# Batch 1's transposes in PSUM tiles of their own, and its visits moved: block-causal attention with a gated FFN on one core

## The chip, the cores and the metric

The kernel runs on one core of a Trainium2 chip. The metric is device time in microseconds (us), the median of several runs of the same program. A core has a matrix engine (PE, with a separate weight load, PEld), a vector engine (DVE), an activation engine (ACT), a general engine (POOL) and a synchronisation engine (SP) that here only issues DMAs. The engines run side by side; each takes its own instructions in order, and they wait for one another on semaphores. Matmul results land in PSUM, which DVE and ACT empty into the on-chip SBUF.

## The reference

```
q, k, v: [8 batches, 8 heads, 576, 64] f32
scores = q @ k^T / 8, masked so that a row of block i (64 rows) sees blocks j <= i
attn   = softmax(scores);  o = attn @ v
x      = o as [8*576, 512]                   # heads side by side
out    = (relu(x @ w_gate) * (x @ w_val)) @ w_out   # 512 -> 1536 -> 512, f32 out
```

## The kernel before, in words

**Tiling.** A batch has 576 rows: four chunks of 128 (the "mains") and a tail of 64. The FFN takes 512 rows of a batch at a time (the four chunks), with a ninth pass at the end for the tails of all eight batches. Heads go in pairs: round `r` is batch `r // 4`, pair `hp = r % 4`. All matmuls are bf16.

**One long FFN, with attention set into it.** `ffn_gen` (L579) is a generator that issues one 512-column FFN matmul at each step: for each batch 96 steps of gate and val products (L585; 12 column blocks `f`, four gate and four val matmuls each, then a relu on ACT, L595, and a product on DVE, L601, which gives `hT`), then 48 steps of output products (L646; four groups of 12, each copied to `ob` by DVE, L656, and stored). A batch of FFN is 144 steps. Around it the order is written out by hand: `run(base, events)` (L796) sorts a list of (position, function) and issues FFN steps up to the whole part of each position before it calls the function. So position 96 means: after FFN step 95 of this batch. The order of every engine's instructions is the order of these calls; no scheduler changes it.

**A visit** (L381) is the attention of one round: scores of the four chunks in three parts. The third part has a half in a `one` tile and a half in an `ffnp` tile, and the first and second part have an `sc` tile each. Three exponentials on ACT follow (L410 for the third part, L404 for the other two; the last one at a position of its own). `corners` (L459) zeroes masked corners, `head_av` (L517) multiplies one head's weights with v (10 matmuls, L508) and normalises on DVE (L473, L474), and `to_xT_pe` (L546) transposes the result for the FFN.

**PSUM** has three pools: `psum_sc` with two tiles of [128, 2, 512] f32 (`sc`), `psum_one` with one tile (`one`), and `psum_ffn` with three tiles (`ffnp`). A tile that is asked for waits until the last reader of the buffer's former tile is done. `ffnp` serves the gate and val products, the output groups, half of each third part, the products with v and the transposes of x; so those share three buffers.

**Batch 1's q and k** have to be transposed before its visits (rounds 4 to 7). While batch 0's FFN runs, POOL, DVE and ACT cast them to bf16 (L168), and `pe_mains` (L232) transposes one head pair on PE: four 128x128 transposes for q and four for k (L239) into PSUM, then one cast for each into `qTm` and `kTm` (L248), q on DVE and k on ACT. For pairs 0 to 2, `mains_1` (L868) hands in one `sc` tile whose two halves hold q and k; for pair 3 `pe_mains` takes two `ffnp` tiles. Round 4 + hp needs the casts of pair hp.

Positions before: pair 0 at 91, pair 1 at 92, visit of round 4 at 96, of round 5 at 112, round 4's products with v at 120, pair 2 at 122, round 4's x transposes at 125, visit of round 6 at 126, round 5's products at 128, pair 3 at 130, round 5's x transposes at 132, visit of round 7 at 138. At position 128 `mains_2(0)` also starts casts on POOL and loads on SP for batch 2, which is transposed by DMA and put in order by `un` (L856).

Of the kernel before, what the change touches and what calls it, by code (L numbers as in the profile page):

```python
# [11 lines left out]
BF = mybir.dt.bfloat16  # L12
# [5 lines left out]
def kernel(  # L18
# [26 lines left out]
    psum_sc = ctx.enter_context(  # L45
        tc.tile_pool(name="psum_sc", bufs=2, space=bass.MemoryType.PSUM)
    )
    psum_one = ctx.enter_context(
        tc.tile_pool(name="psum_one", bufs=1, space=bass.MemoryType.PSUM)
    )  # L50
# [287 lines left out]
    def cast_w(sts, eng):  # L338
        for dst, st in sts:
            eng(dst, st)  # L340
# [40 lines left out]
    def visit(r):  # L381

        b, hp = divmod(r, 4)
        at = attnT[r % 4]
        first = psum_sc.tile([128, 2, 512], FP, name="sc")
        second = psum_sc.tile([128, 2, 512], FP, name="sc")
        third = thirds()
        for c, hh in [(c, hh) for c in (2, 0, 1, 3) for hh in range(2)]:
            where = {
                0: first[:, hh, :],  # L390
                1: second[:, hh, 0:384],
                3: second[:, hh, 384:512],
                2: third[hh],
            }
            nc.tensor.matmul(  # L395
                where[c].rearrange("p (c n) -> p c n", n=128),
                kTm[b % 2][head_of(hh), c, hp, :],
                qTm[b % 2][head_of(hh), c:4, hp, :],
                start=True,
                stop=True,  # L400
            )

        def exp(sc, lo):
            return lambda: nc.scalar.activation(  # L404
                at[:, :, lo : lo + 512], sc, AF.Exp, scale=scale
            )

        def exp_third():
            for hh in range(2):
                nc.scalar.activation(  # L410
                    at[:, hh, 1024:1280], third[hh], AF.Exp, scale=scale
                )

        return exp_third, exp(first, 0), exp(second, 512)
# [44 lines left out]
    def corners(r, zero):  # L459

        at = attnT[r % 4]
        for lo, n in ((0, 512), (896, 128)):
            two = at[64:128, :, lo : lo + 2 * n].rearrange("p g (c n) -> p g c n", c=2)
            zero(two[:, :, :, 0:64])
# [4 lines left out]
    def normalise(out, av):  # L469
        n = av.shape[1]  # L470
        rows = av.shape[0]
        recip = sb.tile([128, NCH], FP, name="recip", bufs=4)[0:rows, 0:n]
        nc.vector.reciprocal(recip, av[:, :, 64])  # L473
        nc.vector.tensor_tensor(  # L474
            out=out,
            in0=av[:, :, 0:64],
            in1=recip.to_broadcast([rows, n, 64]),
            op=AX.mult,
        )
# [24 lines left out]
    def products_with_v(b, h, at, av):  # L504
        for p in range(4):
            for c in range(p + 1):
                col = BASE[c] + 128 * (p - c)
                nc.tensor.matmul(  # L508
                    av[:, p, :],
                    at[:, col : col + 128],  # L510
                    v_bf[b % 2][:, c, h, :],
                    start=(p == 0),
                    stop=(c == p),
                    skip_group_check=True,
                )

    def head_av(r, hh):  # L517
        b, hp = divmod(r, 4)
        h = 2 * hp + hh
        at = attnT[r % 4]  # L520
        if hh == 0:
            xnats[r] = sb.tile([128, 4, 128], BF, name="xnat", bufs=3)
        xnat = xnats[r]
        if b > 0 or hh == 1:
            av = psum_ffn.tile([128, 4, 65], FP, name="ffnp")
        else:
            av = psum_one.tile([128, 4, 65], FP, name="one")
        products_with_v(b, h, at[:, hh, :], av)
        normalise(xnat[:, :, 64 * hh : 64 * hh + 64], av)

    def both_av(r):

        b, hp = divmod(r, 4)
        xnats[r] = sb.tile([128, 4, 128], BF, name="xnat", bufs=3)
        for hh in range(2):
            sc = psum_sc.tile([128, 2, 512], FP, name="sc")
            av = sc[:, 0, 0:260].rearrange("q (p e) -> q p e", e=65)
            products_with_v(b, 2 * hp + hh, attnT[r % 4][:, hh, :], av)
            normalise(xnats[r][:, :, 64 * hh : 64 * hh + 64], av)
# [155 lines left out]
    dve, act, pool = nc.vector.tensor_copy, nc.scalar.copy, nc.gpsimd.tensor_copy  # L695
# [7 lines left out]
    with tc.manual_schedule(engines={E.PE, E.DVE, E.Activation, E.Pool, E.SP}):  # L703
# [28 lines left out]
        part(2, 0)  # L732
        part(2, 1)
        head_av(0, 0)
        head_av(0, 1)
        part(2, 2)
        e0.cast_v(4, 2, pool)
        corners(2, zero_pool)
        head_av(1, 0)
        part(3, 0)  # L740
        to_xT_pe(0, dve)
# [19 lines left out]
        e1, e2 = Early(1), Early(2)  # L761
# [39 lines left out]
        def round_at(p, r, av, to_xT, after=(6, 13)):  # L801

            exps = []

            def begin():
                exps.extend(visit(r))
                exps[0]()
                exps[1]()

            return [  # L810
                (p, begin),
                (p + after[0], lambda: exps[2]()),
                (min(p + after[1], av[0] - 0.5), lambda: corners(r, zero_dve)),
                *(
                    [(av[0], lambda: both_av(r))]
                    if av[1] is None
                    else [(av[i], lambda i=i: head_av(r, i)) for i in range(2)]
                ),
                (to_xT[0], lambda: to_xT[1](r)),
            ]  # L820

        def tail_at(p, b, av):
            exps = []
            x = sb.tile([64, 512], BF, name="xtail", bufs=2)

            def begin():
                exps.extend(tail_visit(b))
                exps[0]()
                exps[1]()

            def end():
                tail_av(b, 1, x)
                tail_to_xT(b, x)

            return [
                (p, begin),
                (p + 6, lambda: exps[2]()),
                (av[0], lambda: tail_av(b, 0, x)),
                (av[1], end),
            ]  # L840
# [18 lines left out]
        def mains_2(h0):  # L859
            e2.load_v_chunks(h0 // 4)  # L860
            e2.cast_qk(h0, 4, (pool, pool))
            e2.transpose(h0 // 4)
# [2 lines left out]
            e2.load_tails((0, 1))  # L865
            e2.load_tails((2,))

        def mains_1(hp, evac=(dve, act)):  # L868
            two = psum_sc.tile([128, 2, 1024], BF, name="sc")
            e1.pe_mains(hp, evac, [two[:, t, 0:512] for t in range(2)])  # L870

        events = round_at(96, 4, (120, 120.1), (125, pe_xT), (6, 11))
        events += round_at(112, 5, (128, 128.1), (132, pe_xT), (4, 14))
        events += round_at(126, 6, (138.2, 139), (146, pe_xT), (4, 9))
        events += round_at(138, 7, (148, None), (153, pe_xT), (3, 8))
        events += [
            (67, lambda: cast_w(halves[1:], act)),
            (80, lambda: e1.cast_qk(0, 4, (None, dve))),
            (91, lambda: mains_1(0)),
            (92.5, lambda: mains_1(1)),  # L880
            (112.05, lambda: cast_w(last_w[1:], dve)),
            (122.5, lambda: mains_1(2)),
            (130, lambda: e1.pe_mains(3, (dve, act))),
            (128, lambda: mains_2(0)),
            (142, lambda: e0.pe_tails((dve, act))),
            (142, lambda: e1.pe_tails((dve, act))),
# [4 lines left out]
        events = tail_at(24, 0, (37, 39)) + tail_at(40, 1, (55, 58))  # L891
# [15 lines left out]
        for b in range(3, B):  # L907
            events = tail_at(120, b, (136, 140))
            if b == 3:
                events += tail_at(3, 2, (21, 25))  # L910
            for i, p in enumerate((27, 50, 73, 96) if b == 3 else (2, 32, 62, 92)):
                r = 4 * b + i
# [43 lines left out]
```

The softmax here doesn't subtract the row's maximum and nothing guards it: scores larger than these inputs give would overflow.

## Time and profile before

| what | value |
|---|---|
| median of five runs | 366.93 us (366.25 to 367.38) |
| profiled execution, its own time | 367.36 us |
| its span in the profile | 365.3 us |
| busy: PE, DVE, ACT, POOL | 98%, 46%, 46%, 31% of the span |
| granted TensorE clock | 1.00 |
| share of PE in the chain that ended last | 96% |

The profile shows one execution. A line of the timeline has the start (us from the span's start), the duration, the engine, the source line, the operation, what it writes and reads, how many instructions were merged, and in brackets the idle time before it and what released it. Matmuls are pipelined: one of 512 columns takes 0.38 us from start to end, but the next starts 0.22 us after it, so PE's rows overlap, and "busy 98%" does not mean that PE never stood still. A wait of PE shows as a start that comes later than the pitch of the matmuls ahead of it gives. The table of waits counts only idle time between rows, so it gives less than the true standing of PE; it does give the name of what was waited for.

### The profile page before, as it was taken

What the parts mean: (1) busy time and instruction counts of PE and PEld (TensorE: products, weight loads), DVE (VectorE), ACT (ScalarE), POOL (GpSimd) and SP (SyncE); (2) the same over time, 40 slices, a digit from 0 to 9 for tenths busy, and PEclk for the clock granted to TensorE, in tenths of its full rate; (3) what the DMA queues carried; (4) which work ended last, traced back from release to release, by engine and by line L of the source; (5) the groups of instructions that cost most, each with busy time, mean ns of one, the idle gap of its engine ahead of it and who ended that gap; (6) DMA issues with size and microseconds to landing.
All of it is one profiled execution on the core that took longest, in us unless ns stands there. A gap on an engine that the chain in (4) does not pass through costs nothing.

```text
span 365.3 us, 7455 instructions
## 1 busy us (share of the span) xinstructions
PE 357.0 (98%) x2963; PEld 176.9 (48%) x2963; DVE 168.3 (46%) x393; ACT 168.5 (46%) x278; POOL 113.7 (31%) x147
## 2 busy tenths in 40 slices
PE   7999999999999999999999999999999999999995
PEld 3544445554554545444544455445544454444443
DVE  4753555465535544454354534553355434333332
ACT  4834565577245733664256634554455333302310
POOL 5676656399119100760058002900000000000000
PEclk9999999999999999999999999999999999999999
DMA  8999999999999972999369982998100320020013
GB/s 253 286 357 373 315 243 300 237 98 134 145 197 137 149 149 80 76 123 187 117 45 149 144 140 49 141 134 158 64 17 14 74 81 0 0 88 29 0 45 102
DMA packets 150339, 49.58 MB, mean 136 GB/s; under 512 B 132768, under 2 KB 143264, under 8 KB 150304
## 3 DMA queue, kind: packets, MB, share of 16 engines
q0 software_dynamic: 70320, 8.85, 51.7%
q1 hardware_dynamic: 74704, 31.08, 42.6%
q10 hardware_dynamic: 5280, 9.18, 7.9%
q8 instruction: 23, 0.38, 0.4%
q14 instruction: 12, 0.10, 0.1%
HBM read 37.75 MB, written 9.44 MB: 129 GB/s over the span
## 4 chain that ended last, share of the span: by engine, by line
PE 96%; DVE 2%; ACT 1%; issue 0%; POOL 0%; ACTq 0%; POOLq 0%
PE ffnp L585 51%; PE ffnp L646 26%; PE ffnp L508 5%; PE sc L395 3%; PE ffnp L488 3%; PE one L395 2%; PE sc L352 1%; PE sc L429 1%; PE ffnp L239 1%; PE ffnp L691 1%; DVE qTm L248 1%; PE sc L585 0%; PE one L429 0%; PE one L508 0%; DVE xnat L474 0%
## 5 line engine op out<-in xcount | busy, mean ns | idle before, releaser
L601 DVE TENSOR_TENSOR hT<-gate_sb,ffnp 128x512 bf16<-128x512 bf16 x106 | 72.8, 687 | 95.5 <-PE ffnp L585 75.4
L595 ACT ACTIVATE gate_sb<-ffnp 128x512 bf16<-128x512 f32 x108 | 64.7, 601 | 100.6 <-PE ffnp L585 100.6
L585 PE MATMUL ffnp<-xT,wg 128*128 128x512 bf16 x384 | 103.7, 379 | 0.1
L646 PE MATMUL ffnp<-wo,hT 128*128 128x512 bf16 (+1 forms) x444 | 101.4, 373 | 0.2 <-DVE ob L656 0.2
L585 PE MATMUL ffnp<-xT,wv 128*128 128x512 bf16 x376 | 101.0, 379 | 0.0
L585 PEld LDWEIGHTS <-wg 128*128 128x128 bf16 x432 | 40.2, 98 | 46.3 <-issue 4.0
L585 PEld LDWEIGHTS <-wv 128*128 128x128 bf16 x432 | 39.9, 98 | 45.5 <-issue 2.3
L646 PEld LDWEIGHTS <-hT 128*128 128x128 bf16 x444 | 40.9, 98 | 42.0 <-issue 1.1
L404 ACT ACTIVATE attnT<-sc 128x1024 bf16<-128x1024 f32 x56 | 56.9, 1039 | 0.0
L282 POOL DMA_DIRECT2D q_bf<-in_q_dram x20 | 17.7, 902 | 94.8 <-DVE hT L601 79.9
L656 DVE COPY ob<-ffnp 128x512 f32<-128x512 f32 (+1 forms) x37 | 25.0, 677 | 41.5 <-PE ffnp L646 41.5
L508 PEld LDWEIGHTS <-attnT 128*128 128x128 bf16 x640 | 26.0, 98 | 14.5 <-DVE xnat L474 3.8
L473 DVE RECIPROCAL recip<-ffnp 128x4 f32<-128x4 f32 (+1 forms) x73 | 13.1, 179 | 35.5 <-PE ffnp L508 23.4
L508 PE MATMUL ffnp<-v_bf,attnT 128*128 128x65 bf16 x570 | 26.4, 194 | 0.0
L410 ACT ACTIVATE attnT<-one 128x256 bf16<-128x256 f32 x28 | 10.8, 384 | 32.6 <-PE ffnp L395 30.1
L474 DVE TENSOR_TENSOR xnat<-ffnp,recip 128x256 bf16<-128x256 f32 x57 | 24.2, 424 | 2.0
L282 POOL DMA_DIRECT2D v_bf<-in_v_dram x25 | 21.4, 932 | 0.2 <-PE ffnp L508 0.2
L450 ACT ACTIVATE attnTt<-one 64x256 bf16<-64x256 f32 x8 | 3.0, 377 | 36.0 <-PE ffnp L429 36.0
L282 POOL DMA_DIRECT2D k_bf<-in_k_dram x20 | 17.7, 939 | 0.0
L395 PE MATMUL sc<-qTm,kTm 64*128 64x512 bf16 (+1 forms) x168 | 17.2, 305 | 0.4 <-ACT kTm L248 0.4
L395 PEld LDWEIGHTS <-kTm 64*128 64x128 bf16 x224 | 9.2, 94 | 16.2 <-issue 11.7
L441 ACT ACTIVATE attnTt<-sc 128x1024 bf16<-128x1024 f32 x16 | 15.7, 1014 | 0.0
(89 smaller groups left out, 244.9 us busy)
## 6 DMA issues: line engine op xcount, KB each, us to landing
out_dram<-ob ACTq DMA_DIRECT2D x32, 256.0 KB, 2.9
stage<-in_moe_w_gate_dram SPq DMA_DIRECT2D x6, 512.0 KB, 9.3
stage<-in_moe_w_val_dram SPq DMA_DIRECT2D x6, 512.0 KB, 9.6
stage<-in_moe_w_out_dram SPq DMA_DIRECT2D x6, 512.0 KB, 10.3
q_bf<-in_q_dram POOLq DMA_DIRECT2D x20, 128.0 KB, 4.7
k_bf<-in_k_dram POOLq DMA_DIRECT2D x20, 128.0 KB, 5.5
v_bf<-in_v_dram POOLq DMA_DIRECT2D x20, 128.0 KB, 6.3
stage<-in_v_dram SPq DMA_DIRECT2D x19, 128.0 KB, 4.8
```

Of the source, the lines that this page charges most:

```text
L282: ins = nc.gpsimd.dma_start(dst, src[b, :, 128 * c : 128 * c + n, :].rearrange("h p d -> p h d"),)
L395: nc.tensor.matmul(where[c].rearrange("p (c n) -> p c n", n=128), kTm[b % 2][head_of(hh), c, hp, :], qTm[b % 2][head_of(hh), c:4, hp, :], ...
L404: return lambda: nc.scalar.activation(at[:, :, lo : lo + 512], sc, AF.Exp, scale=scale)
L441: return lambda: nc.scalar.activation(at[:, :, 2 * i : 2 * i + 2, 0:256], main[i].rearrange("p g (h n) -> p g h n", h=2), AF.Exp, scale=scale,
L473: nc.vector.reciprocal(recip, av[:, :, 64])
L474: nc.vector.tensor_tensor(out=out, in0=av[:, :, 0:64], in1=recip.to_broadcast([rows, n, 64]), op=AX.mult,)
L508: nc.tensor.matmul(av[:, p, :], at[:, col : col + 128], v_bf[b % 2][:, c, h, :], start=(p == 0), stop=(c == p), skip_group_check=True,)
L585: nc.tensor.matmul(to, (wg, wv)[t][f // 4][:, c, 128 * (f % 4) : 128 * (f % 4) + 128], x[:, c], start=(c == 0), stop=(c == 3),)
L595: nc.scalar.activation(gate_sb, gate, AF.Relu)
L601: nc.vector.tensor_tensor(out=h, in0=gate_sb, in1=val, op=AX.mult)
L646: nc.tensor.matmul(op, hT[f][:, 128 * s : 128 * (s + 1)], wo[f // 4][:, f % 4, n0:n1], start=(f == 0), stop=(f == 11),)
L656: nc.vector.tensor_copy(ob, op)
```

## The change

- Pairs 0 to 2: q and k get a PSUM tile each instead of the halves of one `sc` tile: pair 0's q in `one`, its k and both of pairs 1 and 2 in `sc` tiles. Pair 3 leaves `ffnp`: its q and k lie side by side in one `one` tile (a single bank).
- Positions: pairs 0 to 3 at 89, 91, 121.5 and 128.5 instead of 91, 92.5, 122.5 and 130. Round 5's products with v at 129 instead of 128 and its x transposes at 134 instead of 132. The visit of round 6 at 127 instead of 126 (its last exponential and its corners, whose positions are relative, move by one with it).
- The product with v of round 4's first head is in the `one` tile instead of an `ffnp` tile.

```diff
@@ head_av
-        if b > 0 or hh == 1:
+        if (b > 0 or hh == 1) and (r, hh) != (4, 0):
             av = psum_ffn.tile([128, 4, 65], FP, name="ffnp")
         else:
             av = psum_one.tile([128, 4, 65], FP, name="one")
@@ mains_1 and the list of events
-        def mains_1(hp, evac=(dve, act)):
-            two = psum_sc.tile([128, 2, 1024], BF, name="sc")
-            e1.pe_mains(hp, evac, [two[:, t, 0:512] for t in range(2)])
+        def mains_1(hp):
+            if hp == 3:
+                both = psum_one.tile([128, 1024], BF, name="one")
+                two = [both[:, 512 * t : 512 * t + 512] for t in range(2)]
+            else:
+                two = [
+                    psum_one.tile([128, 1024], BF, name="one")[:, 0:512]
+                    if (hp, t) == (0, 0)
+                    else psum_sc.tile([128, 2, 1024], BF, name="sc")[:, 0, 0:512]
+                    for t in range(2)
+                ]
+            e1.pe_mains(hp, (dve, act), two)
 
         events = round_at(96, 4, (120, 120.1), (125, pe_xT), (6, 11))
-        events += round_at(112, 5, (128, 128.1), (132, pe_xT), (4, 14))
-        events += round_at(126, 6, (138.2, 139), (146, pe_xT), (4, 9))
+        events += round_at(112, 5, (129, 129.1), (134, pe_xT), (4, 14))
+        events += round_at(127, 6, (138.2, 139), (146, pe_xT), (4, 9))
         events += round_at(138, 7, (148, None), (153, pe_xT), (3, 8))
...
-            (91, lambda: mains_1(0)),
-            (92.5, lambda: mains_1(1)),
+            (89, lambda: mains_1(0)),
+            (91, lambda: mains_1(1)),
             (112.05, lambda: cast_w(last_w[1:], dve)),
-            (122.5, lambda: mains_1(2)),
-            (130, lambda: e1.pe_mains(3, (dve, act))),
+            (121.5, lambda: mains_1(2)),
+            (128.5, lambda: mains_1(3)),
             (128, lambda: mains_2(0)),
```

## The prediction, made before the result was known

> **What bounds the kernel now.** I read the page first, then PE's waits, then the chain of waits between 38 and 62 us, then the timeline of that stretch.
>
> ```profile
> span 365.3 us, 7455 instructions
> PE 96%; DVE 2%; ACT 1%; issue 0%; POOL 0%; ACTq 0%; POOLq 0%
> ...
> 299.29 20.72 PE ffnp L585 x96
> ```
>
> PE carries 96% of the chain. The last line is from the chain in order of time: 96 matmuls of 512 columns in 20.72 us, so one starts every 0.216 us. That is my ruler: where PE starts later than its ruler says, it stood still. The change touches only 39 to 61 us (batch 1's visits), and its worth is the standing there. The table of waits names the waits; the timeline gives their sizes.
>
> ```profile
> PE sc L395 <- ACT kTm L248: 0.4, 1, 0.4
> PE one L395 <- ACT kTm L248: 0.3, 1, 0.3
> PE ffnp L646 <- DVE ob L656: 0.2, 1, 0.2
> PE ffnp L239 <- DVE xnat L474: 0.2, 1, 0.2
> ...
> ACT kTm L248 <- DVE qTm L248: 4.4, 2, 2.3
> ```
>
> ```profile
> 39.88 1.35 DVE L248 COPY qTm<-sc 128x512 bf16<-128x512 bf16 x2 [0.34 <-PE sc L239]
> ...
> 40.60 0.59 ACT L248 COPY kTm<-sc 128x512 bf16<-128x512 bf16 x1 [2.09 <-DVE qTm L248]
> ...
> 41.42 0.38 PE L395 MATMUL sc<-qTm,kTm 64*128 64x512 bf16 x2
> 41.57 0.59 ACT L248 COPY kTm<-sc 128x512 bf16<-128x512 bf16 x1
> ...
> 42.22 0.40 PE L395 MATMUL sc<-qTm,kTm 64*128 64x384 bf16 x4 [0.42 <-ACT kTm L248]
> ...
> 48.69 0.69 DVE L656 COPY ob<-ffnp 128x512 f32<-128x512 f32 x1 [0.17 <-PE ffnp L646]
> ...
> 49.44 0.59 PE L646 MATMUL ffnp<-wo,hT 128*128 128x512 bf16 x2 [0.17 <-DVE ob L656]
> ...
> 51.24 0.59 ACT L248 COPY kTm<-sc 128x512 bf16<-128x512 bf16 x1 [2.33 <-DVE qTm L248]
> ...
> 51.88 0.28 PE L395 MATMUL one<-qTm,kTm 64*128 64x256 bf16 x1 [0.32 <-ACT kTm L248]
> ...
> 54.26 0.38 PE L239 MATMUL ffnp<-ident,q_bf 128*128 128x128 bf16 x4
> ...
> 54.80 0.38 PE L239 MATMUL ffnp<-ident,k_bf 128*128 128x128 bf16 x4 [0.16 <-DVE xnat L474]
> ...
> 55.86 1.46 PE L646 MATMUL ffnp<-wo,hT 128*128 128x512 bf16 x6
> ```
>
> The reader is to see that a k cast on ACT starts when the q cast on DVE ends (39.88+0.69=40.57, then 40.60), because both come from one `sc` tile, and that a visit then waits for k. PE's standing by the ruler: 0.58 at 42.22 (the pair at 41.42 is fed by 41.64); 0.33 at 49.44 (20 products from 48.49 at 0.030 end at 49.10; `ob`'s buffer comes free at 49.38); 0.48 at 51.88 (51.18+0.22=51.40); 0.25, 0.33 and 0.18 at 54.26, 54.80 and 55.86 (`ffnp` buffers held by av and by the casts). Sum 2.15 us. Every visit also starts 0.10 late with nothing waiting (55.86+6x0.216=57.16, the start is 57.25); that stays.
>
> **The change part by part.** No instruction is added or removed; SP's and POOL's order is unchanged, and no DMA belongs to a moved step. Costs come from moved waits alone. Positions count FFN matmuls.
>
> *Head pairs 0 and 1* (positions 89 and 91 for 91 and 92). q0 goes to `one`, k0 and the later ones to `sc` tiles of their own. Position 88's matmul starts at 38.58, so q0 runs 38.80-39.02 and k0 to 39.25 (eight transposes take 0.45: 39.23 to 39.68 in the trace). k0's cast waits for PE alone: last transpose 39.19 + 0.26 (the lag of before: 39.62 to 39.88) = 39.45, to 40.04. After two matmuls q1 runs 39.68-39.90. k1 needs the `sc` buffer that k0's cast holds: a new wait, 40.10 - 39.90 = 0.19. No row shows it; at least 0 (if the cast starts at once), at most 0.3 (if k0's cast is tied to q0's DVE cast, which starts at 39.54 behind the hT product). I take 0.19. Behind it on PE queue the gate's last matmul and four val matmuls, and hT, which is no later than now (41.7 against 41.89). k1's cast runs 40.5-41.1, the q casts end at 40.92, and the visit starts at 41.50 with everything free: its second `sc` pair, late by 0.58 now, waits for nothing. Net 0.58 - 0.19 = 0.39.
>
> *(4,0)'s product in `one`.* The out group that follows no longer takes the buffer of the second `ob` copy but of the first (47.83-48.52). 0.33 goes. `one` is free there: its exponential ended at 46.80.
>
> *Head pair 2* (121 for 122), *third visit* (127 for 126). DVE sets the pace: `ob` 48.69-49.38, two av normalisations to 50.47, q cast 50.51-51.20. The k cast now runs beside it, and two more matmuls lie between: PE reaches the visit 0.12 after the q cast. 0.48 - 0.10 = 0.38 goes. POOL's k cast of heads 4 and 5 (47.88-48.50, fed by DMA) is needed at 49.1 instead of 50.0: cover 0.6.
>
> *Head pair 3* (128 for 130), q and k in one bank, (5,0) and (5,1) at 129, xT at 134. With 1.12 gained by then, visit 6 starts at 50.98 and its third exponential leaves `one` at 51.74 (0.38 + 0.38 after the start, as at 51.88 now). PE comes to the transposes at 51.84: no wait, with cover 0.05. The products of (5,0) and (5,1) stand behind them. On DVE the q cast now stands ahead of their normalisations: cast 52.49-53.18, the first done at 53.80, the second at 54.34. The next out group (due 53.76) and the xT transposes (due 54.3) wait for these: I take 0.32 together. Low end 0.1 (if q's cast starts after its own four), high end 0.8 (one cast of 0.69 more). Now 0.25+0.33+0.18 = 0.76, so net 0.44.
>
> *A rule against this part.* Row: at 55.22 the k cast of pair 3 ran beside the q cast (54.68-55.37), from two tiles; pairs 0 to 2 ran one after the other though each half has a bank of its own. The Trainium skill ("PSUM — Partial Sum Buffer", section "PSUM bank collisions raise a hardware error") says that two engines must not touch one bank and quadrant at once, reads included, and that different banks are clean. So the old wait was the tile's, not the bank's, while the new single bank forces ACT behind DVE. By the old row k3's cast would run 52.5-53.1; by the rule 53.2-53.8, and the visit's second 1.04 us exponential behind it on ACT ends at 54.9. The sum is the same by both: the last visit, at 55.7, wants that `sc` buffer at 55.9, cover 1.0. After it ACT has a store to issue (0.35) and xT (0.59) before the last visit's first exponential at 56.1: cover 0.3. Without cover it would cost up to 0.7. The store and a load exchange completion slots; both slots' earlier transfers had been read by 53.2, so 0.
>
> *Behind 61 us* PE is dense. One thing does not move with it: DMA. DVE's third unpermute (76.20) would come at 74.7, and its transfer lands at about 75.1 (landing events). DVE waits 0.5; its next work for PE is the tail's reciprocal, which waits 1.61 for PE (78.40). 0. Batch 3's k lands at 109.3, and its visit comes at 111.8: cover 2.5.
>
> Sum: 0.39+0.33+0.38+0.44 = 1.54. The profiled execution took 367.36 (span 365.3 and 2.06 around it), which becomes 365.8; it lies 0.43 over the median of the five runs, 366.93, which becomes 365.4. With the bounds (0 to 0.3, 0.1 to 0.8) the gain is 1.0 to 1.95, so 365.0 to 365.9; a median's own scatter (runs 366.25 to 367.38) adds some 0.4 either way.
>
> **The rivals.** *A, the gain shrinks*: ACT becomes the pace of visits 6 and 7. For: its 4.5 us of work between third exponentials leaves 0.3. Against: visit 7's products need ACT only 0.65 after its start, as now. If one cast (0.6) and the high ends come true, 0.4 to 0.7 is left: 366.3.
>
> *B, nothing arrives*: PE gains the 1.5, then gives it back at a DMA-fed step (unpermute, batch 3's k). For: the landings are fixed in time. Against: the covers above. 366.9.
>
> *C, slower*: the loads of heads 4 to 7 become the bound. Place: POOL's casts at 47.0 to 50.2, each of which waits 0.2 for its DMA. PE now wants k of pair 2 at 49.1 (done 48.50) and of pair 3 at 52.1 (done 50.18), with two heads' products and an out group queued behind. Price: each us of lateness beyond 0.6, on PE itself, where the old places had 1.5 to 4. It decides from 0.6+1.5 = 2.1 us of lateness; at 3 us, 366.93+0.9 = 367.8. Against: the runs scatter by 1.1 in all.
>
> That the change doesn't do what it says is excluded by the order of instructions: the k casts of pairs 0 to 2 wait for PE, no longer for DVE.
>
> **How the numbers follow.** About 0.2% (0.73 us) is what a measurement of this kernel can tell from no change. The forecast 0.68 (nearly all faster by more), A 0.12 (a third still faster), B 0.09, C 0.11. Faster 0.71, same 0.17, slower 0.12. The forecast's own range is 364.6 to 366.2; with A and a part of B the range is 364.6 to 366.9.
>
> **What would show it.** Right: k casts of pairs 0 to 2 starting within 0.3 of their transposes; about 0.2 of PE standing before k1; none inside visit 4, none before the third out group; visit 6 0.9 us earlier; 0.3 before the fourth out group and the xT transposes; visit 7 at 55.7; afterwards every row of PE 1.5 earlier. Wrong: PE standing over 0.3 at k1, waiting for `one` at pair 3, for POOL's k_bf, or new stops after 61 us.

## The result, and the profile after

The changed kernel took 365.45 us (median of 24 runs, 364.71 to 366.83) beside 366.71 us for the kernel before (median of 45; one of these took 2060 us, and medians are used). The ratio is 0.9962 with a 95% interval of 0.9953 to 0.9971: a gain of 1.39 us (1.06 to 1.72). It is not the quotient of the two medians, which differ by 1.26 us; gains and rises below go by the ratios. The profiled execution took 365.83 us with a span of 364.1 us and a granted clock of 0.995.

The same kernel in another series of runs gave 0.9976 (0.9966 to 0.9987), 0.9 us. The two series differ by more than either interval's half width, so the gain is known as about 0.9 to 1.4 us and no closer.

A part of it lies outside every profile. A run's time less its span is 1.78 us on average in the 25 runs of the changed kernel (1.73 to 1.84) and 1.99 in the 64 runs of before in the other series (1.88 to 2.08). So some 0.2 us of the gain is not the work of any wait on PE. It does not go with the change as such: of the ten kernels below that have the change in whole or in part, six have 1.8 and four 2.0. Its cause is open.

The chain of waits, by engine, on the page of the changed kernel:

```profile
span 364.1 us, 7452 instructions
...
PE 83%; DMA 12%; SPq 1%; POOL 1%; DVE 1%; ACT 1%; issue 0%; ACTq 0%
```

PE carried 96% of this chain before. It now has 83%, and 12% lies on DMA: the chain leaves PE early in the span and runs through loads. That line alone says that transfers, and no engine, now hold a part of the stretch that the change touches. The chain in order of time shows the place (start, duration, engine, what it wrote):

```profile
12.75 8.85 DMA stage<-in_moe_w_val_dram
...
32.03 10.82 DMA stage<-in_moe_w_out_dram
...
45.12 4.83 DMA stage<-in_k_dram
...
50.01 0.62 POOL k_bf L168
...
52.79 5.06 DMA stage<-in_k_dram
...
57.90 0.62 POOL k_bt L178
...
58.57 0.29 PE ffnp L260 x4
```

From 12.75 to 58.57 us PE has no part of this chain: loads of weights and then of k follow one another, with casts and DMA issues between them. The transposes of batch 1's tails (L260) waited for POOL's cast of k's tails, and that cast for a load. PE's table of waits says it in one line (total, times, longest); the four waits that the prediction listed are all gone from it:

```profile
PE ffnp L260 <- POOL k_bt L178: 0.8, 1, 0.8
```

The timeline of the changed kernel, the rows that answer to those shown of before:

```profile
38.76 0.59 ACT L248 COPY kTm<-sc 128x512 bf16<-128x512 bf16 x1 [0.93 <-PE sc L239]
38.77 0.68 DVE L248 COPY qTm<-one 128x512 bf16<-128x512 bf16 x1
...
38.99 0.39 PE L239 MATMUL sc<-ident,q_bf 128*128 128x128 bf16 x4
...
39.40 0.38 PE L239 MATMUL sc<-ident,k_bf 128*128 128x128 bf16 x4
...
40.91 0.60 PE L395 MATMUL sc<-qTm,kTm 64*128 64x512 bf16 x6
...
46.35 1.05 POOL L181 CAST v_bf<-stage 128x1024 bf16<-128x1024 f32 x1 [1.01 <-DMA stage<-in_v_dram]
...
47.46 0.46 PE L508 MATMUL one<-v_bf,attnT 128*128 128x65 bf16 x10
...
47.90 0.62 POOL L168 CAST k_bf<-stage 128x512 bf16<-128x512 f32 x1
...
48.28 0.39 PE L239 MATMUL sc<-ident,q_bf 128*128 128x128 bf16 x4
...
48.58 0.40 PE L239 MATMUL sc<-ident,k_bf 128*128 128x128 bf16 x4
...
50.42 0.28 PE L395 MATMUL one<-qTm,kTm 64*128 64x256 bf16 x1
...
51.95 0.69 DVE L248 COPY qTm<-one 128x512 bf16<-128x512 bf16 x1 [1.59 <-PE one L239]
...
52.67 0.59 ACT L248 COPY kTm<-one 128x512 bf16<-128x512 bf16 x1 [0.29 <-DVE qTm L248]
...
53.79 0.40 PE L554 MATMUL ffnp<-ident,xnat 128*128 128x128 bf16 x4
...
54.98 0.28 PE L395 MATMUL one<-qTm,kTm 64*128 64x256 bf16 x1
...
57.48 0.27 PE L260 MATMUL ffnp<-ident,q_bt 64*128 64x64 bf16 x4
...
57.90 0.61 POOL L178 CAST k_bt<-stage 64x512 bf16<-64x512 f32 x1 [0.49 <-DMA stage<-in_k_dram]
...
58.57 0.29 PE L260 MATMUL ffnp<-ident,k_bt 64*128 64x64 bf16 x4 [0.81 <-POOL k_bt L178]
```

To be seen: pair 0's k cast on ACT starts at 38.76 beside the q cast on DVE (38.77), where it followed that cast before, and the six score products of the first and second part of visit 4 are one row (40.91, x6), where before they were two rows with PE standing between. By the ruler of the prediction (0.216 us a matmul of 512 columns) PE stands 0.18 us at 39.40 (pair 1's k), 0.11 at 53.79 (xT) and 0.97 at 58.57 (k's tails, due at 57.60). The first product with v starts at 47.46, 0.06 after the cast of v (46.35 + 1.05 = 47.40) that it reads. Pair 2's k transposes (48.58) start 0.06 after POOL's cast of that k (47.90 + 0.62 = 48.52), 0.08 later than the ruler gives (48.28 + 0.22 = 48.50).

**One clock for both profiles.** Absolute times mislead here: the code up to position 88 is the same in both kernels, yet position 88's matmul starts at 38.58 in the profile of before and at 37.90 in that of the changed kernel. So I count from that matmul. "Tails" is the first score product of batch 0's tail visit (L429, position 24 of batch 1's FFN), which lies behind everything that the change moves; the last column is from there to the span's end.

| profile | position 88 | visit 4 | visit 5 | visit 6 | visit 7 | tails | rest |
|---|---|---|---|---|---|---|---|
| before | 38.58 | 2.72 | 7.52 | 13.30 | 18.67 | 28.86 | 297.90 |
| changed | 37.90 | 2.90 | 7.10 | 12.53 | 17.09 | 28.24 | 297.92 |
| changed, again | 37.82 | 2.90 | 7.10 | 12.62 | 17.17 | 28.36 | 297.90 |

At visit 7 the changed kernel has gained 18.67 - 17.09 = 1.58 us, which is close to the 1.54 of the prediction. At the tails it has 0.62: 0.96 was given back at L260. Of the 1.28 us between the two spans, 0.68 lies ahead of any changed instruction and is an accident of these two executions. So a time close to the measured one was forecast, and the profile does not yet say why.

### The profile page after: what moved, and what is told of

It reads as the page before. It is cut to its first block, busy times and chain, and to the rows that moved or that the text cites. A ratio compares the mean times of both kernels' runs of the same rounds, so it can differ in the third digit from the quotient of the medians.

```text
span 364.1 us, 7452 instructions
## 1 busy us (share of the span) xinstructions
PE 355.4 (98%) x2963; PEld 176.4 (48%) x2963; DVE 168.2 (46%) x393; ACT 168.9 (46%) x278; POOL 113.7 (31%) x147
## 4 chain that ended last, share of the span: by engine, by line
PE 83%; DMA 12%; SPq 1%; POOL 1%; DVE 1%; ACT 1%; issue 0%; ACTq 0%
PE ffnp L585 46%; PE ffnp L646 23%; PE ffnp L508 4%; DMA stage<-in_moe_w_out_dram 3%; PE sc L395 3%; PE ffnp L488 3%; DMA stage<-in_k_dram 3%; DMA stage<-in_moe_w_gate_dram 3%; DMA stage<-in_moe_w_val_dram 2%; PE one L395 1%; PE sc L429 1%; DMA stage<-in_q_dram 1%; PE ffnp L239 1%; SPq L158 1%; PE one L429 0%; PE sc L352 0%
```

## The experiments

The theory after this reading: the moved waits are worth some 1.6 us on PE, and an execution keeps what DMA-fed casts on POOL leave of it, because PE does not set when these end, and now comes to them earlier. Its rivals: that PE keeps all of it and the stop at L260 is an accident of one execution, and that some parts of the change do nothing or harm. Twelve kernels ran in three series, each beside the kernel before; each expectation is as it was written ahead of its run.

**The same kernel again (`after_again`).** No edit.

> The changed kernel once more, as the measure for the three beside it. Both theories: ratio to before 0.995 to 0.997. In its profile: PE stands about 0.18 us before the k transposes of pair 1 and nothing inside the visit of round 4. Theory T (the tails' k cast, fed by DMA, is now late in most executions): PE stands 0.3 to 1.0 us before the tails' k transposes (L260) here too. Rival S (the one profiled execution was unlucky): under 0.1 us there.

Measured: 365.69 us, ratio 0.9976 (0.9966 to 0.9987). The stop stands in this profile too:

```profile
57.95 0.61 POOL L178 CAST k_bt<-stage 64x512 bf16<-64x512 f32 x1 [0.65 <-DMA stage<-in_k_dram]
...
58.62 0.29 PE L260 MATMUL ffnp<-ident,k_bt 64*128 64x64 bf16 x4 [0.85 <-POOL k_bt L178]
```

It is no accident of one execution.

**The tails' transposes later, in the changed kernel and in the one before (`tails_late`, `before_tails_late`).**

```diff
-            (142, lambda: e1.pe_tails((dve, act))),    # in the list of batch 0's FFN
+            (20, lambda: e1.pe_tails((dve, act))),     # in the list of batch 1's FFN
```

> The changed kernel with batch 1's tail transposes (e1.pe_tails) at position 20 of the next batch's FFN instead of 142, so that PE does not come to them before POOL's cast. T: faster than the changed kernel by 0.3 to 0.9 us (ratio to before 0.994 to 0.9955) and no L260 wait. S: within 0.15 us of the changed kernel (0.996). Should the tile that the transposes take from ffnp between gate and val products cost something, it is slower by up to 0.3.

> The kernel before with batch 1's tail transposes at position 20 of the next batch alone. T and S: in the kernel before PE comes to the tails 1.5 us later, so there is little to win: ratio 0.9985 to 1.0005. If the wait is an old one that also comes in executions of the kernel before, faster by 0.3 us or more (under 0.999).

Measured: 365.74 us, 0.9978 (0.9966 to 0.9990), and 366.77 us, 1.0005 (0.9995 to 1.0015). The kernel before gains 0.2 us at most, so its tails waited for next to nothing. In the changed kernel the stop at L260 is gone from the trace (the transposes run at 63.84), but the time did not move: the expected gain was wrong. The table's columns for it: visit 6 at 12.78, tails at 27.69, rest 298.57. It reached the tails 0.55 earlier than the changed kernel and paid 0.65 behind them. Its waits, its timeline and its chain (last two lines) name the new places:

```profile
PE ffnp L395 <- DVE hT L601: 0.2, 1, 0.2
```

```profile
71.65 2.59 DVE L223 COPY qTm<-perm 128x512 bf16<-128x512 bf16 x2
...
74.89 0.27 PE L395 MATMUL ffnp<-qTm,kTm 64*128 64x256 bf16 x1 [0.18 <-DVE hT L601]
```

```profile
70.50 5.32 DMA perm<-q_bf
...
75.84 0.77 DVE qTm L223
```

Two unpermute copies on DVE took 2.59 us together, where two of before's take 1.11. The hT product behind them freed its `ffnp` buffer late, and visit 8 stood 0.36 us by the ruler. The other 0.3 us went between visit 8 and visit 9, where the chain runs through the transfer that the third unpermute reads (landed at 75.82). In this execution the lead that one DMA-fed step no longer ate was eaten behind it.

**Pair 1 one position later (`k1_at_92`)**, which should remove the wait that the change brings at pair 1's k.

```diff
-            (91, lambda: mains_1(1)),
+            (92, lambda: mains_1(1)),
```

> The changed kernel with pair 1's transposes one FFN matmul later (92 for 91). By the prediction's step the new wait before k1 (0.19 by the sum, 0.18 in the trace) goes and nothing takes its place: 0.18 us faster than the changed kernel, hardly clear of noise in time, but the row must show it. Rival: ACT takes the relu of the last gate first, so k1's cast ends 0.6 later and the second sc pair of the visit of round 4 waits again, 0.1 to 0.4 us: same or slower.

Measured: 365.73 us, 0.9973 (0.9964 to 0.9983). Visit 4 stands at 2.72 instead of 2.90, so the 0.18 is gone from its place, as expected; the time, with an interval of 0.35 us either way, can't show it. PE's waits in this execution:

```profile
PE ffnp L260 <- POOL k_bt L178: 0.5, 1, 0.5
...
PE one L508 <- POOL v_bf L181: 0.2, 1, 0.2
```

**Each part undone (`undo_pairs01`, `undo_av`, `undo_pair2`, `undo_pair3`)**, the rest of the change kept.

```diff
# undo_pairs01: pairs 0 and 1 share one sc tile again, at 91 and 92.5
+            elif hp in (0, 1):
+                pair = psum_sc.tile([128, 2, 1024], BF, name="sc")
+                two = [pair[:, t, 0:512] for t in range(2)]
# undo_av: round 4's first product with v in ffnp again
-        if (b > 0 or hh == 1) and (r, hh) != (4, 0):
+        if b > 0 or hh == 1:
# undo_pair2: pair 2 shares one sc tile again, at 122.5; visit of round 6 at 126
# undo_pair3: pair 3 in two ffnp tiles again, at 130
+            (130, lambda: e1.pe_mains(3, (dve, act))),
#   and round 5's products at 128, its x transposes at 132
```

> The changed kernel with pairs 0 and 1 as before (q and k as the halves of one sc tile, at 91 and 92.5). By the prediction's sum this gives back 0.39 us: ratio to before about 0.9973 where the changed kernel has 0.9962; the trace shows 0.58 us of standing inside the visit of round 4 and none before k1. Rival (the gain came from elsewhere, the placing of these pairs is hidden): 0.9962.

> The changed kernel with round 4's first product with v in ffnp again. By the sum: 0.33 us of standing comes back before the third out group, ratio 0.9971. Rival: with that tile back in ffnp the order of ffnp buffers shifts for what follows, and the wait turns up later or not at all: 0.9962, or over 0.9975.

> The changed kernel with pair 2 in one sc tile at 122.5 and the visit of round 6 at 126, as before. By the sum 0.38 us comes back before that visit (ratio 0.9973). Rival: pair 3, which now follows two positions behind the visit, takes up a part of it, since its wait for the normalisations is then covered: 0.1 to 0.2 us net (0.9966).

> The changed kernel with pair 3 as before (two ffnp tiles, position 130; round 5's products at 128, its x transposes at 132). By the sum 0.44 us comes back (0.25, 0.33 and 0.18 of standing for 0.32): ratio 0.9974. In the trace of the changed kernel only 0.11 of the 0.32 is left, so if that reading is right the loss is up to 0.65 us (0.9980). Rival: the waits for the tails behind it absorb the loss, 0.9962.

Measured, each with 22 runs beside 367.18 us of before: 366.29 us, 0.9982 (0.9971 to 0.9993); 365.84 us, 0.9958 (0.9942 to 0.9973); 366.46 us, 0.9981 (0.9966 to 0.9995); 366.23 us, 0.9978 (0.9967 to 0.9989). Against the first series of the full change (0.9962) all but `undo_av` lie clearly higher; against the second (0.9976) none does, and the full change did not run in their series. `undo_av` shows no loss at all, though its expected 0.9971 is still inside its interval; and `undo_pair2` and `undo_pair3` have 0.2 us more outside the span than the full change (2.00 and 1.97 for 1.78). With intervals of 0.4 to 0.6 us either way, a part of 0.3 to 0.6 us is too small for the time. The traces tell it. Each has its old wait back, at its place (one line each, in the order above):

```profile
41.34 0.40 PE L395 MATMUL sc<-qTm,kTm 64*128 64x384 bf16 x4 [0.42 <-ACT kTm L248]
```

```profile
49.72 0.38 PE L646 MATMUL ffnp<-wo,hT 128*128 128x512 bf16 x1 [0.17 <-DVE ob L656]
```

```profile
50.26 0.28 PE L395 MATMUL one<-qTm,kTm 64*128 64x256 bf16 x1 [0.47 <-ACT kTm L248]
```

```profile
53.34 0.38 PE L239 MATMUL ffnp<-ident,k_bf 128*128 128x128 bf16 x4 [0.17 <-DVE xnat L474]
```

So the rival that some part does nothing falls as far as the trace goes: every part takes away the wait that it was said to take away. What each is worth in the median stays open.

**PE held back (`before_pe_delay`, `after_pe_delay`).** Five matmuls of 512 columns are added at position 84, 1.08 us by the ruler; nobody reads their result. If the time is PE's, it rises by that; if a DMA-fed cast waits further on, the delay is swallowed by that wait.

```diff
+        def pe_delay():
+            jp = psum_one.tile([128, 512], FP, name="one")
+            for _ in range(5):
+                nc.tensor.matmul(jp, ident, zeros, start=True, stop=True)
...
+            (84, lambda: pe_delay()),
```

> The kernel before with five extra 512-column matmuls on PE (into the free one tile, never read) at position 84, ahead of everything that the change touches: PE comes 1.08 us later to every step behind. Theory D (in the changed kernel the DMA-fed casts, whose times are fixed by the loads, have become the next bound; in the kernel before they have room): here nothing absorbs the delay, so slower by 0.9 to 1.1 us (ratio 1.0025 to 1.003). Rival E (DMA-fed steps bind neither kernel): the same, 1.08.

> The changed kernel with the same five extra matmuls. D: the waits for POOL's v cast and for the tails' k cast shrink by what PE comes later (0.1 to 0.2 and up to 1.0), so the total rises by only 0.1 to 0.5 us over the changed kernel: ratio to before 0.997 to 0.999. E: it rises by 1.08 us, ratio 0.9995 to 1.000. In the trace: by D no wait before the tails' k transposes, and the first tail visit comes at most 0.5 us later than in the changed kernel (66.1); by E 1.1 later.

Measured: before rose from 366.67 to 367.65 us, 1.0032 (1.0017 to 1.0047): 1.17 us with an interval of 0.6 to 1.7, so the delay came out in full as far as the noise tells. The changed kernel with the delay took 366.30 us, 0.9988 (0.9977 to 0.9999). Against its two ratios without it (0.9962 and 0.9976) that is a rise of 1.0 or 0.4 us. Some 0.24 us of this lies outside the span (2.02 for 1.78); the spans alone rose by 0.67 or 0.39 us on average, where before's rose by 1.11. So a part seems to be swallowed, but the intervals do not exclude that all of it is passed on. The profile: position 88 at 38.96, visits at 2.89, 7.10, 12.38 and 16.94, tails at 27.14. Its timeline:

```profile
45.93 1.05 POOL L181 CAST v_bf<-stage 128x1024 bf16<-128x1024 f32 x1 [1.38 <-DMA stage<-in_v_dram]
...
48.45 0.47 PE L508 MATMUL one<-v_bf,attnT 128*128 128x65 bf16 x10
...
56.78 0.61 POOL L178 CAST k_bt<-stage 64x512 bf16<-64x512 f32 x1
...
58.40 0.27 PE L260 MATMUL ffnp<-ident,q_bt 64*128 64x64 bf16 x4
...
58.52 0.28 PE L260 MATMUL ffnp<-ident,k_bt 64*128 64x64 bf16 x4
```

PE comes 1.06 us later than in the changed kernel's profile and finds both casts done, at 46.98 and 57.39. With nothing in PE's way, the change shows its whole worth: 28.86 - 27.14 = 1.72 us. The tails come at 66.10 absolute, where the undelayed kernel has 37.90 + 28.24 = 66.14; but this is not a delay seen being swallowed. In this execution the casts also ended earlier (there 47.40 and 58.51), and PE without its delay would have come to k's tails at 57.46, just behind the cast too.

What holds these transposes shows across the eight profiles that have the change in whole or in part and keep them at 142. In five (the changed kernel twice, `k1_at_92`, `undo_pairs01`, `undo_pair2`) k's transposes start 0.05 to 0.06 us after POOL's cast ends, which is at 57.76 to 58.72. In three (`after_pe_delay`, `undo_av`, `undo_pair3`) the cast had ended before PE came, and they start 0.11 to 0.12 behind q's. Whichever is later sets the start.

Behind the tails `after_pe_delay` loses 0.36 (rest 298.28), most of it (0.28) at visit 8 as `tails_late` did:

```profile
72.60 2.53 DVE L223 COPY qTm<-perm 128x512 bf16<-128x512 bf16 x2
73.25 1.43 POOL L189 CAST v_bf<-stage 128x1024 bf16<-128x1024 f32 x1
75.05 0.68 DVE L601 TENSOR_TENSOR hT<-gate_sb,ffnp 128x512 bf16<-128x512 bf16 x1
...
75.78 0.27 PE L395 MATMUL ffnp<-qTm,kTm 64*128 64x256 bf16 x1
```

**Both retouches together (`combined`), and with v's load behind the transposes by DMA (`combined_sp`).** `combined` is `tails_late` with pair 1 at 92. `combined_sp` also moves one load on SP, so that the unpermutes' transfers start earlier:

```diff
         def mains_2(h0):
-            e2.load_v_chunks(h0 // 4)
+            if h0 == 4:
+                e2.load_v_chunks(1)
             e2.cast_qk(h0, 4, (pool, pool))
             e2.transpose(h0 // 4)
+            if h0 == 0:
+                e2.load_v_chunks(0)
```

> The changed kernel with pair 1 at 92 and batch 1's tail transposes at position 20 of the next batch: both waits that the changed kernel's trace shows are gone. If only those waits stood in the way: 0.5 to 1.1 us faster than the changed kernel (ratio 0.994 to 0.9955). By D the lead is given back at the next DMA-fed step, batch 2's unpermute at 72 to 76 us: within 0.3 us of the changed kernel (0.996 to 0.9975).

> The one before with batch 2's first v chunks issued on SP behind the first two DMA transposes instead of ahead of them, so that the transposes start about 1 us earlier (in the kernel before SP spends 57.2 to 61.5 us on those loads, and POOL's cast that the transposes need is done at 60.4). D: the unpermute is no longer late and the lead of 0.5 to 1.0 us reaches the end: ratio 0.994 to 0.996, the fastest of all. Rival: the transposes wait for the same DMA engines and land no earlier, or v lands late for POOL: like the one before, or slower.

Measured: `combined` 365.21 us, 0.9957 (0.9943 to 0.9972), six runs; its profile has the shortest span of all profiles, 362.9 us, visits at 2.72, 6.93, 12.20 and 16.76, tails at 27.11, rest 298.01. Here v's cast came in time:

```profile
45.94 1.05 POOL L181 CAST v_bf<-stage 128x1024 bf16<-128x1024 f32 x1 [0.93 <-DMA stage<-in_v_dram]
...
47.14 0.47 PE L508 MATMUL one<-v_bf,attnT 128*128 128x65 bf16 x10
```

It is the fastest version measured, but its interval overlaps that of the change, so that it beats it is possible and not shown. `combined_sp` took 365.80 us, 0.9973 (0.9962 to 0.9983). In its profile the unpermutes ran at their usual length (median 0.596 us), as hoped, but the first product with v, whose load is not the one that was moved, started at 47.40, right behind its cast, and tails came at 27.66; the time is no better than `combined`, and the two intervals overlap. The move of the load settles nothing.

## Why the prediction was right, point by point

- **Sum 1.54 us.** Up to visit 7 it held (1.58). In the execution where nothing DMA-fed stood in the way (`after_pe_delay`) the moved waits were worth 1.72 us, in `combined` 1.75, of which 0.18 is pair 1's retouch and not the change's. By part, from its visits (visit 6 has one matmul more ahead of it, 0.22): pairs 0 and 1 are 7.52 - 7.10 = 0.42 (said 0.39); the product in `one` with pair 2 is 0.92 + 0.22 - 0.42 = 0.72 (said 0.33 + 0.38); pair 3 is 1.73 - 0.92 - 0.22 = 0.59 (said 0.44).
- **The wait at pair 1's k, 0.19.** Right: 0.18.
- **Pair 3, "I take 0.32 together".** Too much: 0.11, all at the xT transposes; the fourth out group waited for nothing. This is the term that was mis-sized. The order that it rested on held: k's cast from the single bank starts at 52.67, when q's ends (51.95 + 0.69), visit 7 was not held by it, and `one` was free at the transposes. That the bank and not the tile made k wait was not tried: both are one here.
- **Covers.** One that was named was used up: POOL's k cast of heads 4 and 5 was to be needed at 49.1, with a cover of 0.6, but PE came at 48.50, before it had ended (48.52). That cost 0.08. Two covers were not named at all, and so priced at zero. One is POOL's cast of v ahead of round 4's first product: it costs some 0.1 us in the changed kernel's profile. The other is POOL's cast of k's tails ahead of L260. In the profile of before no wait showed there:

```profile
57.06 0.61 POOL L178 CAST k_bt<-stage 64x512 bf16<-64x512 f32 x1
...
59.86 0.28 PE L260 MATMUL ffnp<-ident,k_bt 64*128 64x64 bf16 x4
```

  The cast ended at 57.67, and PE came 2.2 us behind it. But the change brings PE 1.6 us earlier; that execution had PE 0.7 us late at position 88 (38.58, where ten of the other eleven profiles without a delay have 37.46 to 37.90); and in the changed kernel's profile the cast ended 0.84 later, at 58.51. Over all 14 profiles it ended between 57.4 and 58.7. Together these used up the cover, and it cost 0.97 us. This is the step that failed: covers left out, or read from one execution.
- **"Behind 61 us PE is dense", the unpermutes at 0.** Right for the profiled execution (rest 297.92 against 297.90), wrong as a rule. From visit 8 to visit 9 both take 5.01 us, but five of the other kernels 5.22 to 5.68. In `tails_late` (5.68) and `after_pe_delay` (5.40) visit 8 itself stood, by 0.36 and 0.28, behind unpermute copies that ran beside POOL's. The cover of batch 3's k held, though in before's trace that visit starts at 111.52 and not at 111.8, so it was 2.2 and not 2.5.
- **The rivals.** A did not come: ACT paces no visit. B's mechanism, the gain given back at a DMA-fed step, is real, but for a part of the gain, and in the changed kernel's profile at places that the prediction did not look at; at the unpermute that B named it came only in `tails_late`. C's bound, POOL's casts of heads 4 to 7, held PE in the changed kernel's profile for the 0.08 us at pair 2's k alone, and did not decide.
- **Why the time came out right.** In part by luck. The forecast of 365.4 was counted from 366.93, the median of five runs, where 45 runs of before have 366.71. As a gain, 1.54 was forecast, and 1.39 and 0.9 came. The 2.06 us around the span were taken as given, but the changed kernel has 1.78. Inside the span the gain is thus some 1.2 us in the first series (an estimate, 1.39 - 0.2) and 0.8 in the second (364.79 - 364.02 on average): half to some three quarters of the sum. The worth on PE is a little larger than forecast (1.7), and a part is given back that differs from one execution to the next: 1.0 at L260 in the changed kernel's profile, nothing there in `after_pe_delay`. That the medians are a mean over such executions is argued and fits; it isn't shown, since each profile is one execution and the runs without one don't tell where PE stood.

## What to carry to other kernels

Before a gain on the busiest engine is booked, list every load-fed step that this engine reaches behind it, up to the place where it was waiting anyway, and take the cover of each from the latest landing and the earliest arrival that several profiles show, not from one. Here the same cast ended at times 1.3 us apart. Compare two profiles from a common instruction ahead of the change, not from the span's start: here more than half of the difference of the spans lay ahead of the first changed instruction. A delay put in on purpose can tell whose the time is, but compare it over many runs: in a single profile the wait that should swallow it may be missing by chance, as it was here. And look at the time outside the span before all of a small gain is put down to waits.

## What was not expected of the hardware

Copies on DVE and POOL that met grew, and it was not always the same side. The four unpermute copies of one shape on DVE (count, then min, median and max in ns), in before, in the changed kernel, and in `tails_late`:

```profile
L223 DVE COPY qTm<-perm x4: 586/590/593, 73.9 to 79.5; 128x512 bf16<-128x512 bf16 x4
```

```profile
L223 DVE COPY qTm<-perm x4: 584/591/1096, 72.6 to 78.2; 128x512 bf16<-128x512 bf16 x4
```

```profile
L223 DVE COPY qTm<-perm x4: 767/1115/1493, 71.6 to 77.7; 128x512 bf16<-128x512 bf16 x4
```

With POOL idle such a copy takes 0.59 us (the first two of `combined_sp`). In `tails_late` the first two met POOL's copies of about 1.07 us and took 1.18 and 1.49, and POOL's second copy grew too, to 1.47. In before the first two also met POOL's work and kept their 0.59; there it was POOL's two casts of v, 1.04 us each where nothing meets them, that took 3.02 together:

```profile
72.94 3.02 POOL L189 CAST v_bf<-stage 128x1024 bf16<-128x1024 f32 x2
...
73.94 1.11 DVE L223 COPY qTm<-perm 128x512 bf16<-128x512 bf16 x2
```

The Trainium skill ("SBUF — State Buffer", section "Who interferes with whom") says that DVE's copies can enter a mode in which they take a port that POOL shares, and that the second to come then waits for the whole of the first. The sizes fit: 1.49 is 0.59 and 0.90 more, less than one POOL copy, and POOL's 3.02 is two casts and 0.94 more, less than two DVE copies. That this is the cause was not tried by itself. What matters for this kernel is that a change in PE's times also moves DVE's copies, and so changes which copies meet.
